# Loading the first tokens of a fused SSM and FFN kernel in two column groups, and turning them in smaller pieces

## The chip, the cores and the metric

The kernel runs on one core of one Trainium2 chip. The metric is the device time of one execution in microseconds (us), taken over several runs. All times "from the start" below are microseconds after the beginning of the span of one profiled execution. Every kernel told of here gave a correct result.

## The reference

`x` has 2048 tokens of 640 features, in bf16. A gate mixes a diagonal state-space model with a feed-forward network:

```python
g = sigmoid((x * gate_w).sum(-1, keepdims=True))
a = A_ref(x, ...)      # SSM with 640 complex states: h[t] = Lam_bar*h[t-1] + B_bar x[t];  y = 2 Re(C h) + D x
h = gelu(x @ w1 + b1)  # w1: 640 x 1728
b = h @ w2 + b2        # w2: 1728 x 640
out = g * a + (1 - g) * b
```

## The kernel before

The tokens are worked off in four chunks of 512. A chunk is four tiles of 128 tokens (`a` = 0 to 3), and the 640 features are five blocks of 128 (`kd` = 0 to 4). The first matrix product of the FFN needs x with features on the partitions. For chunks 1 to 3 a DMA transposes x. For chunk 0 TensorE itself "turns" it: each 128x128 block is multiplied by an identity matrix into a `bank` (a tile in PSUM, the memory that matmuls write to), and VectorE (DVE) or ScalarE (ACT) copies it to `xT[0]`. In this document x0, x1, x2, x3 are the four tiles of chunk 0. `w1a`, `w1b` and `w1c` are the first 768, the next and the last columns of w1. The matmuls on w1a are the work of the first 12 us. They are cut into strips so that they can begin when only some tiles and some feature blocks are there.

The start of the kernel (cuts are marked, the comments are mine):

```python
    load_xn(0, 0, 1)                 # x0, all 640 features, SyncE's queue
    load_w1a(nc.scalar, 0)           # ScalarE's queue
    load_xn(0, 1, 2)                 # x1
    load_w1a(nc.scalar, 2)
    ...                              # two parameter rows on ScalarE's queue
    load_xn(0, 2, 3)
    load_xn(0, 3, 4)
    rows(nc.sync, prmA[2 * KS:3 * KS, :], A_Lambda_re)
    for kd in (1, 4, 3):
        load_w1a(nc.sync, kd)
    ...
    pA = bank()
    for n in (512, 512, 512, 512, 512, 512, 128, 128):      # warm-up matmuls on constants
        nc.tensor.matmul(pA[:, 0:n], lhsT=ones(P), rhs=ones(n), start=True, stop=True)
    ...
    tA, tB = bank(), bank()
    turn(tA, 0, 0, 0)                        # turn(bank, column, tile a, block kd)
    turned(nc.vector, tA, 0, 0, 0, 1)        # copy blocks 0..1 of tile 0 to xT[0]
    for i in range(2):
        turn(tB, i * P, 0, 1 + i)
    turned(nc.vector, tB, 0, 0, 1, 3)
    for i in range(2):
        turn(pA, i * P, 0, 3 + i)
    turned(nc.scalar, pA, 0, 0, 3, 5)
    ...
    strip(0, 0, P, True)                     # six matmuls: block 0, tile 0
    turn_all(1)                              # five turns of tile 1, three copies
    strip(2, 0, P, False)
    strip(0, P, HT, True)
    strip(2, P, HT, False, 0, 3)
    turn_all(2)
    ...
```

A simple model of the clock of each engine (`Clock.pe = 4.2`, the moment at which TensorE's work begins) decides in which order DVE's work is issued later on.

## Time and profile before

| | before |
|---|---|
| median of 3 runs | 215.99 us (215.8 to 216.4) |
| span of the profiled execution | 214.2 us |
| TensorE busy | 98% of the span |
| first turn / first w1a matmul / first w1b matmul | 3.60 / 4.22 / 12.82 us |
| DVE's sine tables ready | 25.7 us |

From the page of the kernel before, the length of the span, the busy time of each engine, and the chain of work that ended last by engine:

```profile
span 214.2 us, 3547 instructions
...
PE 210.0 (98%) x1385; PEld 116.4 (54%) x1385; DVE 188.4 (88%) x385; ACT 103.3 (48%) x185; POOL 1.1 (0%) x12
...
PE 96%; DMA 2%; SPq 0%; ACT 0%; DVE 0%; issue 0%
```

TensorE (PE) bounds the kernel. There is almost nothing to win but the holes at the start. These are in the timeline of PE for the first 13 us; the columns are start, length, engine, line, operation, tiles, shapes, count, and in brackets the idle time before and what ended it:

```profile
0.77 2.93 PE L220 MATMUL bank<-const-bfloat16-1.0 128*128 128x512 bf16 x8 [0.77 <-PEq L716]
3.60 0.46 PE L223 MATMUL bank<-ident,xn 128*128 128x128 bf16 x5
4.22 0.49 PE L258 MATMUL bank<-xT,w1a 128*128 128x128 bf16 x6 [0.16 <-DVE xT L230]
4.96 0.45 PE L223 MATMUL bank<-ident,xn 128*128 128x128 bf16 x5 [0.24 <-DMA xn<-in_A_x_dram]
5.25 1.09 PE L258 MATMUL bank<-xT,w1a 128*128 128x128 bf16 x15
...
7.09 0.17 PE L361 MATMUL bank<-ident,prmA 128*128 128x15 bf16 x1 [0.30 <-ACT xT L232]
...
12.82 0.38 PE L258 MATMUL bank<-xT,w1b 128*128 128x512 bf16 x1
```

Read it so: the warm-up matmuls hold PE to about 3.6 us. Then x0 is turned, and PE waits three times, for DVE's copy, for the DMA of x1, and for ScalarE's copy. After that the brackets show no further wait.

The bracket understates a stop, because a matmul is recorded as longer than the distance to the next start. In a full stream a 128-column matmul starts 55 to 56 ns after the one before it and a 512-column one 216 ns after. I therefore call "stop" the distance between two starts less that figure.

DVE's trigonometric work begins with this operation (timeline of DVE, the same columns):

```profile
8.29 0.82 DVE L370 TENSOR_TENSOR gel<-tf,thp_c 128x640 f32<-128x640 f32 x1
```

It is DVE's first operation on 640 columns; the change halves it.

### The profile page before, as it was taken

How to read it: one execution, taken by the hardware profiler on the slowest of the kernel's cores; microseconds unless marked ns; L12 is line 12 of the kernel's file. 1: busy time of each engine (PE TensorE's matmuls, PEld its weight loads, DVE VectorE, ACT ScalarE, POOL GpSimd, SP SyncE). 2: the span in 40 equal slices, each digit the busy share in tenths (PEclk: the TensorE clock that was granted, in tenths of full speed). 3: DMA queues.
4: the chain of work that ended last, by engine and by line, in shares of the span. 5: the costliest groups of instructions: out<-in, count | busy, mean ns of one | idle time of the engine just before them, and what ended most of it. 6: DMA issues, size and time to landing. Idle time of an engine off the chain costs nothing.

```text
span 214.2 us, 3547 instructions
## 1 busy us (share of the span) xinstructions
PE 210.0 (98%) x1385; PEld 116.4 (54%) x1385; DVE 188.4 (88%) x385; ACT 103.3 (48%) x185; POOL 1.1 (0%) x12
## 2 busy tenths in 40 slices
PE   7999999999999999999999999999999999999994
PEld 3745444454454644775445577444455567664773
DVE  2899999999998999998999999899999999973153
ACT  3599956675867697203573210456682422304200
POOL 1000000000000000000000000000000000000000
PEclk9999999999999999999999999999999999999999
DMA  6899999995000000061000006100000000100011
GB/s 200 238 189 182 187 250 314 257 212 136 3 0 0 3 0 2 12 186 62 0 0 3 0 0 185 63 0 0 2 3 14 0 3 31 61 34 0 0 66 61
DMA packets 31059, 15.84 MB, mean 74 GB/s; under 512 B 22978, under 2 KB 31042, under 8 KB 31042
## 3 DMA queue, kind: packets, MB, share of 16 engines
q1 hardware_dynamic: 30590, 15.18, 29.1%
q10 hardware_dynamic: 452, 0.43, 0.6%
q8 instruction: 11, 0.18, 0.3%
q14 instruction: 6, 0.05, 0.1%
HBM read 7.48 MB, written 2.62 MB: 47 GB/s over the span
## 4 chain that ended last, share of the span: by engine, by line
PE 96%; DMA 2%; SPq 0%; ACT 0%; DVE 0%; issue 0%
PE bank L598 27%; PE bank L258 26%; PE bank L657 20%; PE bank L540 20%; DMA xn<-in_A_x_dram 2%; PE bank L614 1%; PE bank L284 1%; PE bank L223 0%; SPq L122 0%; ACT xT L232 0%; DVE ot L662 0%; PE bank L361 0%; PE bank L274 0%; PE bank L390 0%
## 5 line engine op out<-in xcount | busy, mean ns | idle before, releaser
L598 PE MATMUL bank<-w_sb,gel 128*128 128x512 bf16 (+1 forms) x416 | 57.9, 299 | 0.0
L598 PEld LDWEIGHTS <-gel 128*128 128x128 bf16 x416 | 32.3, 98 | 25.5
L543 ACT ACTIVATE bu<-bank 128x512 bf16<-128x512 f32 x40 | 23.6, 608 | 37.3 <-PE bank L540 36.7
L263 ACT ACTIVATE gel<-bank,colB 128x512 bf16<-128x512 f32 x52 | 33.9, 696 | 11.7 <-PE bank L258 11.4
L657 PEld LDWEIGHTS <-hs 128*128 128x128 bf16 x330 | 31.6, 98 | 11.5
L494 DVE TENSOR_TENSOR_SCAN g<-r_c,carry,v 128x512 bf16<-128x512 f32 x30 | 37.3, 1271 | 0.0
L606 ACT ACTIVATE gb<-bank,gcol 128x512 f32<-128x512 f32 (+1 forms) x32 | 15.1, 527 | 33.5 <-PE bank L614 17.3
L258 PE MATMUL bank<-xT,w1a 128*128 128x512 bf16 (+1 forms) x156 | 27.6, 329 | 0.2 <-DVE xT L230 0.2
L657 PE MATMUL bank<-CT_im,hs 128*128 128x320 bf16 (+2 forms) x165 | 27.1, 295 | 0.0
L657 PE MATMUL bank<-CT_re,hs 128*128 128x320 bf16 (+2 forms) x165 | 27.1, 295 | 0.0
L662 DVE SCALAR_TENSOR_TENSOR ot<-bank,gcol,gb 128x320 bf16<-128x320 f32 (+2 forms) x33 | 17.6, 535 | 10.8 <-PE bank L657 10.0
L540 PE MATMUL bank<-xT,BT_re 128*128 128x512 bf16 x100 | 24.8, 379 | 0.0
L540 PE MATMUL bank<-xT,BT_im 128*128 128x512 bf16 x100 | 24.8, 379 | 0.0
L258 PEld LDWEIGHTS <-w1a 128*128 128x128 bf16 x156 | 13.4, 97 | 13.0 <-issue 0.7
L573 DVE TENSOR_TENSOR bank<-xn,Dbc 128x320 f32<-128x320 bf16 (+2 forms) x33 | 14.6, 483 | 3.9 <-ACT gb L606 3.8
L258 PE MATMUL bank<-xT,w1b 128*128 128x512 bf16 x80 | 17.9, 379 | 0.0
L540 PEld LDWEIGHTS <-BT_im 128*128 128x128 bf16 x100 | 9.8, 98 | 11.8
L475 DVE TENSOR_TENSOR v<-wa,wb 128x512 bf16<-128x512 bf16 x40 | 15.2, 421 | 0.6
L540 PEld LDWEIGHTS <-BT_re 128*128 128x128 bf16 x100 | 9.7, 98 | 11.0
L587 ACT ACTIVATE bank<-b2bc 128x512 f32<-128x512 bf16 (+1 forms) x24 | 11.7, 529 | 7.3 <-DVE ot L662 7.3
L475 DVE TENSOR_TENSOR wa<-TCOS,g 128x1024 bf16<-128x1024 bf16 x20 | 13.7, 686 | 0.1
L258 PE MATMUL bank<-xT,w1c 128*128 128x512 bf16 x60 | 13.7, 379 | 0.0
(101 smaller groups left out, 164.2 us busy)
## 6 DMA issues: line engine op xcount, KB each, us to landing
out_dram<-ot SPq DMA_DIRECT2D x15, 160.0 KB, 1.8
w_sb<-in_B_w_dram SPq DMA_DIRECT2D x1, 2080.0 KB
xn<-in_A_x_dram SPq DMA_DIRECT2D x2, 640.0 KB
xn<-in_A_x_dram SPq DMA_DIRECT2D x4, 160.0 KB, 3.7
w1b<-in_B_w_dram SPq DMA_DIRECT2D x5, 128.0 KB, 3.1
xn<-in_A_x_dram SPq DMA_DIRECT2D x2, 320.0 KB, 3.7
w1a<-in_B_w_dram SPq DMA_DIRECT2D x3, 192.0 KB, 3.0
w1c<-in_B_w_dram SPq DMA_DIRECT2D x5, 112.0 KB, 3.5
```

The lines of the kernel that those rows point to most:

```text
L258: nc.tensor.matmul(p[:, t0:t1], lhsT=w, rhs=xT[c][:, kd, t0:t1], start=(kd == 0) if first is None else first, stop=(kd == last), skip_grou ...
L263: nc.scalar.activation(out=gel[c][:, kf, :], in_=p[:, :], func=ACT.Gelu_apprx_tanh, bias=b1_c[:, kf:kf + 1])
L475: nc.vector.tensor_tensor(out=o, in0=a, in1=b, op=op)
L494: nc.vector.tensor_tensor_scan(s["g"][:, ri, :], r_c[:, ks:ks + 1].to_broadcast([P, CH]), s["v"][:, ri, :], init, ALU.mult, ALU.add)
L540: nc.tensor.matmul(p[:], lhsT=BT[ks >= KSA][:, kd, (ks % KSA if ks < KSA else ks - KSA) * P:][:, 0:P], rhs=xT[c][:, kd, :], start=(kd == 0 ...
L543: nc.scalar.activation(out=bu[:, ri, :], in_=p[:], func=ACT.Identity)
L573: dve_now(ck.pe, 0.45, lambda: nc.vector.tensor_tensor(out=p[:, 0:d1 - d0], in0=xn[c][:, a, d0:d1], in1=Dbc[:, d0:d1], op=ALU.mult))
L587: nc.scalar.activation(out=v, in_=src, func=ACT.Identity)
L598: nc.tensor.matmul(p[:, col:col + d1 - d0], lhsT=gel[c][:, kf, a * P:(a + 1) * P], rhs=w2_sb[:, kf, d0:d1], start=False, stop=False, skip_ ...
L606: nc.scalar.activation(out=gbs[ti][:, d0:d1], in_=p[:, col:col + d1 - d0], func=ACT.Identity, scale=gcol[:, 1, ti:ti + 1])
L657: nc.tensor.matmul(p[:, 0:d1 - d0], lhsT=hs[c][:, j, lo:lo + P], rhs=CT[:, j % KS, d0:d1], start=False, stop=(j == 2 * KS - 1), skip_group ...
L662: nc.vector.scalar_tensor_tensor(out=ot[:, d0:d1], in0=p[:, 0:d1 - d0], scalar=gcol[:, 0, ti:ti + 1], in1=gbs[ti][:, d0:d1], op0=ALU.mult, ...
```

## The change

The intent is to feed PE sooner. Of each tile, features 0 to 255 come first (64 KB instead of 160 KB), then the other 384 features of two tiles at a time. More of the copies out of PSUM go to ScalarE. The parameter rows leave ScalarE's queue. Sines are computed for 64 positions instead of 128, with one more doubling by the addition theorem. Chunk 3's x also comes in one DMA instead of two (not shown). The core of the diff, with cuts:

```diff
-    load_xn(0, 0, 1)
+    load_x0(nc.sync, 0, 1, 0, KA * P)            # KA = 2: features 0..255 of tile 0
     load_w1a(nc.scalar, 0)
-    load_xn(0, 1, 2)
-    load_w1a(nc.scalar, 2)
+    load_x0(nc.sync, 1, 2, 0, KA * P)
+    load_w1a(nc.scalar, 1)
+    load_x0(nc.sync, 2, 3, 0, KA * P)
+    load_x0(nc.scalar, 0, H, KA * P, D)          # features 256..639 of tiles 0 and 1
+    load_x0(nc.sync, 3, 4, 0, KA * P)
+    load_w1a(nc.sync, 2)
 ...                                              # three parameter rows now on SyncE's queue
+    load_x0(nc.sync, H, TPC, KA * P, D)
+    nc.sync.dma_start(out=w1a34[:], ...)         # w1a 3 and 4 in one DMA
 ...
-    HC = CH // 4
+    HC = CH // 8
 ...
-        pe = 4.2
+        pe = 3.4
 ...
+    def turn_first(a, other):
+        t = bank()
+        turn(t, 0, a, 0)
+        turned(nc.vector, t, 0, a, 0, 1)
+        turn(other, a * P, a, 1)
+        turned(nc.scalar, other, a * P, a, 1, 2)
+
+    turn_first(0, pA)
+    turn_first(1, bank())
 ...
+    part(0, 0)                                   # part(kd, a): six matmuls of block kd, tile a
+    part(0, 1)
+    turn_first(2, pA)
+    part(1, 0)
+    turn_first(3, pA)
+    part(1, 1)
+    part(0, 2)
+    turn_rest(0, ((KA, KD, bank(), nc.scalar),))
+    part(1, 2)
 ...
+    part(0, 3)
+    turn_rest(1, ((KA, KD, bank(), nc.vector),))
+    part(1, 3)
+    turn_rest(2, ((KA, KD, pA, nc.scalar),))
+    part(2, 0)
 ...
+    turn_rest(3, ((KA, KA + 1, bank(), nc.vector), (KA + 1, KD, pA, nc.scalar)))
 ...
+    part(2, 1)
+    part(2, 2)
+    part(2, 3)
 ...
-    double(HC, 3)
+    double(HC, 4)
+    double(2 * HC, 3)
```

More of the change, by code (lines that the diff above doesn't have):

```diff
@@ L83 @@
     xT = [const.tile([P, KD, CH], BF16, name=f"xT{c}") for c in range(NCH)]
-    w1a = [const.tile([P, cut1], BF16, name=f"w1a_{kd}") for kd in range(KD)]
+    w1a = [const.tile([P, cut1], BF16, name=f"w1a_{kd}") for kd in range(3)]
+    w1a34 = const.tile([P, 2, cut1], BF16, name="w1a34")
+    w1a += [w1a34[:, j, :] for j in range(2)]
     w1b = [const.tile([P, cut2 - cut1], BF16, name=f"w1b_{kd}") for kd in range(KD)]
@@ L128, in rows, with load_x0 @@
         queue.dma_start(out=dst, in_=v.rearrange("(j p) -> j p", p=P))
-    load_xn(0, 0, 1)
-    load_w1a(nc.scalar, 0)
-    load_xn(0, 1, 2)
-    load_w1a(nc.scalar, 2)
+    KA = 2
+    xn[0] = xnp.tile([P, TPC, D], BF16, name="xn")
+    def load_x0(queue, a0, a1, d0, d1):
+        queue.dma_start(out=xn[0][:, a0:a1, d0:d1], in_=x2d[a0 * P:a1 * P, d0:d1].rearrange("(a p) d -> p a d", p=P))
+    load_x0(nc.sync, 0, 1, 0, KA * P)
+    load_w1a(nc.scalar, 0)
+    load_x0(nc.sync, 1, 2, 0, KA * P)
[4 more added lines that the diff above has]
+    load_w1a(nc.sync, 2)
     nc.vector.memset(prmA[:], 0.0)
     nc.vector.memset(prmB[:], 0.0)
-    rows(nc.scalar, prmA[0:KS, :], A_log_dt)
-    rows(nc.scalar, prmA[KS:2 * KS, :], A_Lambda_im)
     warm = const.tile([P, 1], F32, name="warm")
     nc.scalar.activation(out=warm[:], in_=nc.const_aps.tensor(1.0, [P, 1], BF16), func=ACT.Exp)
-    load_xn(0, 2, 3)
-    load_xn(0, 3, 4)
+    rows(nc.sync, prmA[0:KS, :], A_log_dt)
+    rows(nc.sync, prmA[KS:2 * KS, :], A_Lambda_im)
     rows(nc.sync, prmA[2 * KS:3 * KS, :], A_Lambda_re)
-    for kd in (1, 4, 3):
-        load_w1a(nc.sync, kd)
+    load_x0(nc.sync, H, TPC, KA * P, D)
+    nc.sync.dma_start(out=w1a34[:], in_=B_w1[3 * P:KD * P, 0:cut1].rearrange("(k p) f -> p k f", p=P))
     rows(nc.sync, prmB[KS:NB, :], B_b1[0:(KF - 1) * P])
@@ L155 @@
     nc.gpsimd.memset(b1x[:, F_LAST:F_LAST + 1], 0.0)
-    NQ = 4
+    NQ = 5
     spans = const.tile([P, NQ], F32, name="spans")
-    for i, m in enumerate((1.0, float(CH), float(CH // 2), float(CH // 4))):
+    for i, m in enumerate((1.0, float(CH), float(CH // 2), float(CH // 4), float(CH // 8))):
         nc.gpsimd.memset(spans[:, i:i + 1], m)
@@ L232, in turned @@
             nc.scalar.activation(out=dst, in_=src, func=ACT.Identity)
-    tA, tB = bank(), bank()
-    turn(tA, 0, 0, 0)
-    turned(nc.vector, tA, 0, 0, 0, 1)
-    for i in range(2):
-        turn(tB, i * P, 0, 1 + i)
-    turned(nc.vector, tB, 0, 0, 1, 3)
-    for i in range(2):
-        turn(pA, i * P, 0, 3 + i)
-    turned(nc.scalar, pA, 0, 0, 3, 5)
+    def turn_first(a, other):
[6 more added lines that the diff above has]
+    turn_first(1, bank())
     def col(name, dtype=F32, n=KS):
@@ L318, in strip, with turn_rest @@
             ff1_mm(banks[kf], 0, kf, kd, t0, t1, first, 3)
-    def turn_all(a, last=False):
-        tB = bank()
-        for i in range(3):
-            turn(tB, i * P, a, i)
-        turned(nc.vector, tB, 0, a, 0, 1)
-        turned(nc.scalar if last else nc.vector, tB, P, a, 1, 3)
-        for i in range(2):
-            turn(pA, i * P, a, 3 + i)
-        if not last:
-            turned(nc.scalar, pA, 0, a, 3, 5)
+    def turn_rest(a, parts):
+        for k0, k1, t, engine in parts:
+            for k in range(k0, k1):
+                turn(t, (k - k0) * P, a, k)
+            turned(engine, t, 0, a, k0, k1)
     HB = CH // 2
@@ L352, in over, with part @@
         return c.rearrange("p (k o) -> p k o", o=1).to_broadcast([P, KS, n])
-    strip(0, 0, P, True)
-    turn_all(1)
-    strip(2, 0, P, False)
-    strip(0, P, HT, True)
-    strip(2, P, HT, False, 0, 3)
-    turn_all(2)
-    strip(2, P, HT, False, 3, FA)
-    nc.tensor.matmul(pA[:, HT:HT + 3 * KS], lhsT=prmA[:], rhs=ident[:, 0:3 * KS], start=True, stop=True, skip_group_check=True)
-    nc.vector.tensor_copy(out=colA[:], in_=pA[:, HT:HT + 3 * KS])
+    def part(kd, a):
+        strip(kd, a * P, (a + 1) * P, kd == 0)
+    part(0, 0)
[7 more added lines that the diff above has]
+    part(1, 2)
+    nc.tensor.matmul(pA[:, 0:3 * KS], lhsT=prmA[:], rhs=ident[:, 0:3 * KS], start=True, stop=True, skip_group_check=True)
+    nc.vector.tensor_copy(out=colA[:], in_=pA[:, 0:3 * KS])
     nc.scalar.activation(out=dt16[:], in_=ldt_c, func=ACT.Exp)
     nc.vector.tensor_scalar(out=limp[:], in0=lim_c, scalar1=INV_2PI, scalar2=None, op0=ALU.mult)
-    strip(0, HT, HT + P, True)
-    turn_all(3, True)
+    part(0, 3)
[3 more added lines that the diff above has]
+    part(2, 0)
     nc.vector.tensor_tensor(out=dtl[:], in0=dt16[:], in1=lre_c, op=ALU.mult)
     nc.vector.tensor_tensor(out=thp_c[:], in0=dt16[:], in1=limp[:], op=ALU.mult)
+    turn_rest(3, ((KA, KA + 1, bank(), nc.vector), (KA + 1, KD, pA, nc.scalar)))
     nc.scalar.activation(out=r_c[:], in_=dtl[:], func=ACT.Exp)
     nc.vector.tensor_tensor(out=u, in0=tf[:].rearrange("p (o i) -> p o i", o=1).to_broadcast([P, KS, HC]), in1=over(thp_c[:], HC), op=ALU.mult)
-    turned(nc.vector, pA, 0, 3, 3, 5)
     nc.vector.tensor_copy(out=kk[:], in_=u)
     nc.vector.tensor_tensor(out=red, in0=u, in1=kk[:], op=ALU.subtract)
-    strip(2, HT, HT + P, False)
-    strip(0, HT + P, CH, True)
-    strip(2, HT + P, CH, False)
-    strip(1, 0, CH, False)
+    part(2, 1)
+    part(2, 2)
+    part(2, 3)
     nc.scalar.activation(out=FS[:, :, 0:HC], in_=red, func=ACT.Sin, scale=TWO_PI_M)
@@ L690 @@
     fin_a(1)
-    load_xn(3, 0, H)
-    load_xn(3, H, TPC)
+    load_xn(3)
     ssm(3)
```

## The prediction

> **What bounds the kernel now.** TensorE. The page shows PE busy 98% of 214.2 us; the chain that ended last is 96% PE, unbroken from about 7.1 us. Only the start has holes: in the timeline of PE, warm-up matmuls run to about 3.6 us, the first real ones (five turns of tile 0) start at 3.60 when its 160 KB have landed, the first w1a matmul at 4.22, and until 7.1 us PE waits 0.16 (turn copy), 0.24 (second tile's DMA) and 0.30 us (ScalarE copy), about 0.8 us in all. The first w1b matmul starts at 12.82. The change touches the first 13 us: it can win about 1 us.
>
> **What it does, costed.**
> - *First loads.* Tile 0 is 64 KB instead of 160. In the packet records its packets (55 ns each) took from 1.77 to 3.02 us, alternating with w1a's 65 ns packets; landing was 0.5 us later.[...] So smaller x packets (estimate 25 ns) help less than their bytes say: estimate x0 landed at 3.0, x1 at 3.7 (was 4.95). But warm-ups hold PE to about 3.5, and the first w1a matmul stands behind both tiles' turns: 3.8 to 4.0 instead of 4.22.
> - *PE work.* 24 matmuls of 128 columns replace 6 of 512: 24 x 0.06 - 6 x 0.216 = +0.15 us.
> - *Turn buffers.* Most turns share one spare bank and pA, and wait for the copies out of them: gaps of 0.1 us at the third and fourth tiles, about 0.3 us at the last turns (a 384-column copy, 0.5 us, behind only 7 matmuls).
> - *Rows on SyncE, paired w1a.* Their issues wait on earlier landings, but all land before PE needs them.
>
> Sum: first w1b matmul at 12.2 to 12.4: 0.4 to 0.6 us won.
>
> **DVE.** Four ops of 640 columns halve; six of 320 are added.[...] The tables, done at 25.6, will be done 1.5 to 2 us later, though the sines end earlier. DVE has no gap from 15 to 63 us, then gaps of 0.96 (fold), 0.44 and 0.88 us (waits for PE at 92 and 98). These and a changed order of DVE work (the schedule model starts PE 0.8 us earlier) should absorb the lateness before it reaches PE; seeds of the second output stage (1.8 us ahead at 121) are nearest.
>
> **Predicted time.** 215.4 us (215.99 before), 8 in 10 between 214.8 and 216.1. Faster by over 2%: 0.01; within: 0.98; slower: 0.01.
>
> **What will show it.** Timeline of PE: first turn at 3.4 to 3.6, first w1a matmul 3.8 to 4.0, first w1b matmul 12.2 to 12.4, turns waiting for copies about 0.4 us. DVE's tables end at 27 to 27.6. Thereafter every PE piece of the chain of waits keeps its length, shifted alike; PE busy stays near 210.
>
> **What would make it wrong.** The second tile lands before 3.4 us (up to 0.9 won); the spare bank stalls PE more, or ScalarE's turns and table load delay a copy (all lost); DVE's lateness reaches a seed or hs before an output stage (PE gaps at 86 to 98 or 121 to 126 us, up to 1 us slower).

The estimate of 25 ns for a row of 512 B lies on the line through the measured 55 ns for 1280 B and 65 ns for 1536 B. On DVE the terms came to about 1.2 us saved and 2.7 us added; "1.5 to 2 us later" is what is left of them. By the traces a two-tensor fp32 operation takes 0.82 us on 640 columns (before) and 0.48 to 0.49 us on 320 (after), the cast among the four 0.48 and 0.33 us, which makes 1.2 us saved and 2.9 us added. That issues on SyncE's queue wait on earlier landings is in the trace of before: 1.2 us for a w1a block and 0.4 us for an x tile.

## The result

| | before | after |
|---|---|---|
| median of the 4 runs of the same rounds | 215.93 us (215.8 to 216.4) | 216.28 us (215.97 to 216.5) |
| ratio after / before, 95% interval | | 1.0011 (0.9992 to 1.0031) |
| span of the profiled execution | 214.2 us | 214.4 us |
| first turn / first w1a / first w1b | 3.60 / 4.22 / 12.82 us | 3.50 / 4.25 / 13.06 us |
| first w1b matmul to the end of the span | 201.4 us | 201.4 us |
| DVE's tables ready | 25.7 us | 28.5 us |

A ratio here is the mean time of one kernel's fast runs over the mean of the other's fast runs of the same rounds, so it is not quite the ratio of the medians. The change did nothing that can be told from zero; I had expected 215.4. All outputs are right. The page of the kernel after:

```profile
span 214.4 us, 3572 instructions
...
PE 209.4 (98%) x1384; PEld 117.9 (55%) x1403; DVE 189.4 (88%) x389; ACT 103.6 (48%) x188; POOL 1.0 (0%) x13
...
PE 96%; DMA 1%; issue 1%; ACT 0%; SPq 0%; DVE 0%
```

The timeline of PE of the kernel after:

```profile
0.77 2.93 PE L230 MATMUL bank<-const-bfloat16-1.0 128*128 128x512 bf16 x8 [0.77 <-PEq L728]
3.50 0.96 PE L233 MATMUL bank<-ident,xn 128*128 128x128 bf16 x4
4.25 1.49 PE L268 MATMUL bank<-xT,w1a 128*128 128x128 bf16 x12
5.53 0.40 PE L233 MATMUL bank<-ident,xn 128*128 128x128 bf16 x2
...
9.33 0.27 PE L233 MATMUL bank<-ident,xn 128*128 128x128 bf16 x2 [0.19 <-ACT xT L242]
...
13.06 1.24 PE L268 MATMUL bank<-xT,w1b 128*128 128x512 bf16 x5
```

Two things differ from the prediction. The first w1a matmul is at 4.25, not at 3.8 to 4.0, since the second pair of turns (in the group of four at 3.50) starts only at 4.06, when x1 has landed (its DMA has signalled that it is complete). And twelve w1a matmuls take 1.49 us here, while fifteen of them took 1.09 us before. The starts in that group are 107 ns apart. That is half rate, and it lasts to 5.77 us; in the trace of before full rate began at 3.65 us. The column of the granted clock on the page doesn't show this; it reads 9 from the first slice on. The spacing of the matmuls does.

The stop at 9.33 is foreseen (0.3 us) and about right: the distance between the starts is 407 ns, a stop of 0.35. It waits for this copy by ScalarE (timeline of ACT):

```profile
8.79 0.49 ACT L242 ACTIVATE xT<-bank 128x384 bf16<-128x384 f32 x1 [0.62 <-PE bank L233]
```

On DVE, the first of the halved operations starts later than before, since it stands in DVE's order behind the copy of the last but two of the turns (timeline of DVE):

```profile
9.18 0.29 DVE L240 CAST xT<-bank 128x128 bf16<-128x128 f32 x1 [0.19 <-PE bank L233]
9.39 0.48 DVE L384 TENSOR_TENSOR gel<-tf,thp_c 128x320 f32<-128x320 f32 x1
```

From the first w1b matmul to the end of the span both kernels take 201.4 us (214.225 - 12.820 and 214.447 - 13.057). So the tables that DVE finishes 2.8 us later cost nothing, and whatever happened, happened in the first 13 us.

### The profile page after: what moved, and what is told of

Read it like the earlier page. It is cut to its first block, busy times and chain, and to the rows that moved or that the text cites. A ratio compares the mean times of both kernels' runs of the same rounds, so it can differ in the third digit from the quotient of the medians.

```text
span 214.4 us, 3572 instructions
## 1 busy us (share of the span) xinstructions
PE 209.4 (98%) x1384; PEld 117.9 (55%) x1403; DVE 189.4 (88%) x389; ACT 103.6 (48%) x188; POOL 1.0 (0%) x13
## 4 chain that ended last, share of the span: by engine, by line
PE 96%; DMA 1%; issue 1%; ACT 0%; SPq 0%; DVE 0%
PE bank L611 26%; PE bank L268 26%; PE bank L670 20%; PE bank L553 20%; DMA xn<-in_A_x_dram 1%; PE bank L627 1%; PE bank L294 1%; PE bank L233 1%; ACT xT L242 0%; SPq L136 0%; DVE ot L675 0%; PE bank L284 0%; PE bank L402 0%; PE bank L371 0%
## 5 line engine op out<-in xcount | busy, mean ns | idle before, releaser
L611 PE MATMUL bank<-w_sb,gel 128*128 128x128 bf16 (+1 forms) x408 | 57.1, 297 | 0.6 <-issue 0.3
L268 PE MATMUL bank<-xT,w1a 128*128 128x512 bf16 (+1 forms) x170 | 28.2, 318 | 0.2
L268 PEld LDWEIGHTS <-w1a 128*128 128x128 bf16 x174 | 14.8, 102 | 11.4
```

Of the source, the lines that this page charges most:

```text
L268: nc.tensor.matmul(p[:, t0:t1], lhsT=w, rhs=xT[c][:, kd, t0:t1], start=(kd == 0) if first is None else first, stop=(kd == last), skip_grou ...
L611: nc.tensor.matmul(p[:, col:col + d1 - d0], lhsT=gel[c][:, kf, a * P:(a + 1) * P], rhs=w2_sb[:, kf, d0:d1], start=False, stop=False, skip_ ...
```

## The experiments

My first theory was: *the early stage is now cut by waits for copies, and these can be undone (late turn, sines)*. The rivals: *half rate at the start costs the changed kernel more than the kernel before, since it begins real work sooner*; and *the loads do not come sooner, so no order of turns helps*.

### The two kernels again

The same two files, unchanged, on other chips. `after_again` and `before_again`:

> The changed kernel once more, unaltered. Clock theory: the moment when TensorE goes from half to full rate falls at a different place in each execution (5.77 us in the trace on record of after, 3.65 in that of before), and the changed kernel pays about half of every microsecond of delay between 4.1 and 6 us. So if this trace goes to full rate near 3.7 us, its first w1b matmul starts at 12.2 to 12.4 us and the time is about 215.5; at 5.8 us, 13.0 to 13.1 and about 216.3; at 6.8 us, about 13.5 and 216.7. Rival (the new order of loads is slower whatever the clock): first w1b matmul at 13.0 to 13.1 wherever the clock changes.

> The kernel before once more. Clock theory: at 3.7 us its first w1b matmul starts at 12.8 as on record; at 5.8 us at about 13.2, at 6.8 us at about 13.6: it also loses, but less per microsecond, because it waits more for data in that time. Rival: 12.8 wherever the clock changes.

Measured: after 216.15 us (215.56 to 216.65), 0.9992 of before (0.9972 to 1.0012); before against itself 216.33 us, 1.000 (0.998 to 1.002). The spread of one kernel, 1.1 us, is larger than all I look for. In this trace of the changed kernel full rate begins at 3.42 us, and the timeline of PE shows the start without the half rate:

```profile
4.21 0.29 PE L233 MATMUL bank<-ident,xn 128*128 128x128 bf16 x2 [0.46 <-DMA xn<-in_A_x_dram]
4.33 1.08 PE L268 MATMUL bank<-xT,w1a 128*128 128x128 bf16 x12
...
12.67 4.48 PE L268 MATMUL bank<-xT,w1b 128*128 128x512 bf16 x20
```

The same twelve matmuls take 1.08 us instead of 1.49, stop included, and w1b begins 0.39 us sooner than in the trace on record, although w1a began 0.08 later. (The expectation's "half of every microsecond" was an estimate; the trace on record had 1.67 us more of half rate after 4.1 us, and lost 0.39.) So the trace on record was an unlucky one. But x1 is still not there before 4.2 us.

The second trace of *before* is as telling. From its timeline of PE:

```profile
4.28 0.80 PE L258 MATMUL bank<-xT,w1a 128*128 128x128 bf16 x6
4.87 0.58 PE L223 MATMUL bank<-ident,xn 128*128 128x128 bf16 x5
...
12.86 0.38 PE L258 MATMUL bank<-xT,w1b 128*128 128x512 bf16 x1
```

Here half rate lasts to about 5.1 us (by the spacing), the six w1a matmuls take 0.80 us instead of 0.49, and the turns of x1 follow without any wait. x1 landed at 4.43 us here and at 4.91 in the trace on record, though its last row came at 3.98 and 4.03. So the wait of 0.40 us for x1, which the change was to remove, was largely a late landing in the one trace that I had. And w1b begins only 0.04 us later than there, because the slow matmuls fill time that was lost anyway.

A third look at the changed kernel, on yet another chip:

> The changed kernel a third time, so that the next three have it beside them on the same chip. Pooled over the chips so far it is within 0.2 us of the kernel before; I expect that again, with first w1a matmul at 4.2 to 4.35 us.

Measured: 216.10 us (215.97 to 216.20), ratio 1.0005 (0.999 to 1.002). Together the three sets of the changed kernel (15 runs) have a mean of 216.16 us, and the runs of before of the same rounds (26) one of 216.15 us. The difference is 0.0 us; by the spread of the runs it is known to about 0.2 us either way.

This third trace is at full rate from 3.60 us on. PE waits in it for x1 (a stop of 0.38 us) and once more for x2, 0.40 us. From its timeline of PE:

```profile
5.48 0.28 PE L233 MATMUL bank<-ident,xn 128*128 128x128 bf16 x2 [0.24 <-DMA xn<-in_A_x_dram]
```

### The last turns later

```diff
-    turn_rest(3, ((KA, KA + 1, bank(), nc.vector), (KA + 1, KD, pA, nc.scalar)))
+    turn_rest(3, ((KA, KA + 1, bank(), nc.vector),))
 ...
     part(2, 1)
+    turn_rest(3, ((KA + 1, KD, pA, nc.scalar),))
     part(2, 2)
```

> The changed kernel with the last two turns of tile 3 behind six more matmuls of w1a's third part. The trace of after shows PE stopped for 0.35 us there (9.0 to 9.33 us), waiting for ScalarE's copy of 384 columns out of the same bank. If that stop is on the critical path, 0.3 to 0.35 us less than the changed kernel at the same moment of the clock (about 215.9 against 216.27), first w1b matmul 12.7 at 5.8 us. Rival: something later (sines, colB) holds the w1b start, no gain.

Measured: 215.95 us (215.59 to 216.14), ratio 0.9985 (0.9967 to 1.0003). The stop of 0.35 us before the last turns is gone from the timeline of PE, where they now stand at 9.03, and w1b begins at 12.42 us although half rate lasted to 4.86:

```profile
9.03 0.27 PE L233 MATMUL bank<-ident,xn 128*128 128x128 bf16 x2
```

The stop is real and can be avoided by order alone. The median is 0.20 us under `after_again` on the same chip, where I had expected 0.3 to 0.35, and the interval still reaches to 1.

### Sines for 128 positions in the new order

```diff
-    HC = CH // 8
+    HC = CH // 4
 ...
-    double(HC, 4)
-    double(2 * HC, 3)
+    double(HC, 3)
```

> The changed kernel with sines for 128 positions again (one doubling fewer, as before). My theory says that VectorE's work is not on the critical path: the same time as the changed kernel within 0.1 us at the same moment of the clock, though VectorE's tables end about 1.5 us earlier. Rival (VectorE's lateness reaches TensorE somewhere): 0.3 us or more faster.

Measured: 216.38 us (216.19 to 216.56), ratio 1.0002 (0.9985 to 1.0018). I expected no effect on PE, and that was wrong. The timeline of PE:

```profile
12.77 0.38 PE L268 MATMUL bank<-xT,w1b 128*128 128x512 bf16 x1
13.37 4.34 PE L268 MATMUL bank<-xT,w1b 128*128 128x512 bf16 x19 [0.22 <-DVE w1c L405]
```

The second w1b matmul starts 0.60 us after the first instead of 0.22: it needs a bank that DVE has still to empty, and DVE's small copies stand behind the sine work. In all, first w1b to the end of the span took 201.84 us here and 201.4 or 201.5 in every other trace. By this one trace, halving the sines is worth about 0.45 us *in the new order*; the medians on the same chip differ by 0.23. It pays for a delay that the new order itself gives DVE. In the old order 640 columns fitted without a stop.

### Everything on hand before PE begins (a failed design)

I wanted to see the order of PE's work alone. Before the first load I put long memsets on DVE, and gave PE 28 warm-up matmuls of which the second part reads ones from a tile. By mistake I took a tile that a late DMA fills.

```diff
+    wones = Dbc[:, 0:P]
+    nc.vector.memset(w2_sb[:], 0.0)
 ...
+    for n in (512,) * 12:
+        nc.tensor.matmul(pA[:, 0:n], lhsT=wones, rhs=ones(n), start=True, stop=True)
```

> The kernel before with every load held back by about 7 us (by fills on VectorE ahead of them) and the warm-up matmuls made long enough that TensorE is at full rate before the first turn in every execution. About 223 us. If the moment of the clock and nothing else spreads the times of one kernel (215.6 to 216.9 so far), these stay within about 0.3 us of each other; if other things spread them, over 1 us as before. First w1b matmul 12.1 us after the first load's issue (12.82 - 0.73 on record).

> The changed kernel held back in the same way: the comparison of the two without the clock. After_again, at full rate from 3.42 us, started w1b at 12.67 us against 12.82, so I expect first w1b 11.9 to 12.0 us after the first load's issue and 0.1 to 0.2 us less than the held-back kernel before. If the slow clock had taken the whole of my predicted gain, it would be 0.5 to 0.6 us less; if the change is worth nothing, the same.

Measured: 265.27 us (before's order) and 265.36 us (after's). PE stood still until 48.6 and 48.0 us, lost full rate and regained it only at 51.3 and 52.4. The totals answer nothing that was asked. The pair still shows one thing: all loads were long there when PE went on, and from the first turn to the first w1b matmul the old order took 8.78 us and the new one 8.69. With no load to wait for, the two orders differ by 0.1 us in this pair of traces.

### The clock taken out

The same design mended: warm-ups that last until the loads arrive, with ones from a tile that only DVE writes. PE is at full rate from the first turn on: five turns take 0.45 us for before (0.71 in `before_again`, at half rate), and twelve w1a matmuls 1.08 us for after (1.49 in the trace on record).

```diff
+    wones = gelN[0][:, 0, :]
 ...
+    for n in (512,) * 20:
         nc.tensor.matmul(pA[:, 0:n], lhsT=ones(P), rhs=ones(n), start=True, stop=True)
+    for n in (512,) * 12:
+        nc.tensor.matmul(pA[:, 0:n], lhsT=wones, rhs=ones(n), start=True, stop=True)
```

> The held-back kernel before again, with its mistake mended (in the first try the second half of the warm-up read a tile that a late load fills, and TensorE stood still for 40 us). About 223 us. All warm-ups end before the first tile lands and TensorE is at full rate at the first turn. First w1b matmul 12.1 us after the first load's issue. If the moment of the clock is what spreads the times, they now stay within 0.4 us of each other.

> The changed kernel held back in the same way, with the same mending. Clock theory with late x1: w1b 11.9 to 12.0 us after the first load's issue, 0.1 to 0.2 us less than held_before, clear of noise if the spread shrinks. If nothing but the clock took my predicted gain: 0.5 to 0.6 us less. If the loads give nothing: equal.

Measured: 222.94 us (222.72 to 223.40) for before and 223.09 us (223.06 to 223.17) for after, four runs each; ratios 1.0326 and 1.0331. The issue of the first load came at 7.84 us in the one and at 8.02 in the other (the second memset is 592 columns wide in one and 640 in the other), so the 0.15 us between the totals say nothing. Timelines of PE, first of before, then of after:

```profile
10.65 0.45 PE L235 MATMUL bank<-ident,xn 128*128 128x128 bf16 x5
11.27 0.49 PE L270 MATMUL bank<-xT,w1a 128*128 128x128 bf16 x6 [0.16 <-DVE xT L242]
...
19.55 0.81 PE L270 MATMUL bank<-xT,w1b 128*128 128x512 bf16 x3
```

```profile
10.82 0.27 PE L244 MATMUL bank<-ident,xn 128*128 128x128 bf16 x2
11.33 0.29 PE L244 MATMUL bank<-ident,xn 128*128 128x128 bf16 x2 [0.24 <-DMA xn<-in_A_x_dram]
11.45 1.08 PE L279 MATMUL bank<-xT,w1a 128*128 128x128 bf16 x12
...
16.17 0.27 PE L244 MATMUL bank<-ident,xn 128*128 128x128 bf16 x2 [0.19 <-ACT xT L253]
...
19.89 0.38 PE L279 MATMUL bank<-xT,w1b 128*128 128x512 bf16 x1
```

From the issue of the first load, the first w1b matmul comes after 11.71 us in the one and 11.88 in the other. I had expected 0.1 to 0.2 us less for the change, and 0.5 to 0.6 if only the clock had taken its gain. So without the clock the change gains nothing either: the loss of the gain is not the clock's. The stops of these two traces, and of two others that ran at full rate from the first turns on, can be added up, in us:

| stop (distance between starts less the normal one) | before | before, clock held | after again | after, clock held |
|---|---|---|---|---|
| first w1a waits for DVE's copy | 0.32 | 0.32 | 0 | 0 |
| turns of x1 wait for its DMA | 0.40 | 0.09 | 0.62 | 0.40 |
| parameter matmul waits for ScalarE's copy | 0.47 | 0.47 | 0 | 0 |
| sixth w1a matmul waits for ScalarE's copy | 0 | 0 | 0.25 | 0.25 |
| turns of x3 wait for the bank | 0 | 0 | 0.16 | 0 |
| turns of x2 and x3 wait for their DMAs | 0 | 0 | 0 | 0.23 |
| last turns wait for ScalarE's copy | 0 | 0 | 0.35 | 0.35 |
| others | 0.28 | 0.28 | 0.05 | 0.05 |
| sum | 1.47 | 1.16 | 1.43 | 1.28 |

The waits moved, and their sum stayed. In the third trace of the changed kernel it is 1.59, of which 0.79 is for the DMAs of x1 and x2.

### No warm-up matmuls

```diff
-    for n in (512, 512, 512, 512, 512, 512, 128, 128):
-        nc.tensor.matmul(pA[:, 0:n], lhsT=ones(P), rhs=ones(n), start=True, stop=True)
```

> The kernel before without its eight warm-up matmuls. TensorE first works at 3.6 us[...]. I expect about 1 us more than the kernel before (about 217), w1b at about 13.8.

> The changed kernel without warm-up matmuls. Clock theory (the changed kernel gives TensorE dense work from 4.1 us on, and so pays more per microsecond at half rate): 1.2 to 1.4 us more than the changed kernel (about 217.4), 0.2 to 0.4 more than nowarm_before. Rival (both pay alike): the same difference as with warm-ups, 0 to 0.2 us less than nowarm_before.

Measured: before without warm-up 217.47 us (217.29 to 217.78), ratio 1.0071; after without it 217.30 us (216.55 to 217.91), ratio 1.0064. Full rate began at 9.2 and 8.2 us (3.65 and 5.77 in the traces on record). Timeline of PE of the two, first before:

```profile
14.42 0.81 PE L256 MATMUL bank<-xT,w1b 128*128 128x512 bf16 x3
```

```profile
4.35 1.44 PE L266 MATMUL bank<-xT,w1a 128*128 128x128 bf16 x12
...
14.09 4.48 PE L266 MATMUL bank<-xT,w1b 128*128 128x512 bf16 x20
```

Both kernels pay for a late full rate, 1.5 us against before on the same chip and 1.2 us against the changed kernel on other chips. I had expected the changed kernel to come out 0.2 to 0.4 us above the other here, and it came out 0.2 below: my theory that it pays more falls. The clock moved the times of both kernels here; it didn't favour one of them.

### x1 on the other queue

The packet records show why x1 was late. Each tile comes as 128 rows, eight for each of the core's 16 DMA engines if they are spread evenly. The records don't name the tile or the engine of a row; I tell the tiles apart by order.

| | rows of x | time of a row | first to last row of x1 | of w1a's first block |
|---|---|---|---|---|
| before | 1280 B | 55 ns | 2.98 to 4.03 us | 1.93 to 3.34 us |
| after | 512 B | 27 ns | 2.77 to 3.56 us | 1.86 to 3.11 us |
| x1 on the other queue | 512 B | 27 ns | 1.85 to 2.59 us | 2.24 to 3.51 us |

Eight rows of 27 ns are 0.22 us of work, but x1 took 0.79 us. If it shares each engine with w1a on the other queue, whose rows of 1536 B take 65 ns, the sum is 8 x (27 + 65) = 0.74 us. For before, 8 x (55 + 65) = 0.96 us, and it took 1.05. This fits engines that take turns between the two queues. (Whether they do so after each row or after several, the sums don't tell. At the very start it fits less: beside x0 on the other queue x1 took 0.74 us, where 8 x (27 + 27) = 0.43.) So the load of x1 had fewer bytes by 60% but took only 25% less time. And it stood behind x0 on its queue, whose rows beside w1a's took 1.04 us. I moved x1 to 3 to ScalarE's queue, beside x0, and w1a behind x0:

```diff
     load_x0(nc.sync, 0, 1, 0, KA * P)
-    load_w1a(nc.scalar, 0)
-    load_x0(nc.sync, 1, 2, 0, KA * P)
-    load_w1a(nc.scalar, 1)
-    load_x0(nc.sync, 2, 3, 0, KA * P)
-    load_x0(nc.scalar, 0, H, KA * P, D)
-    load_x0(nc.sync, 3, 4, 0, KA * P)
+    load_x0(nc.scalar, 1, 2, 0, KA * P)
+    load_w1a(nc.sync, 0)
+    load_x0(nc.scalar, 2, 3, 0, KA * P)
+    load_w1a(nc.sync, 1)
+    load_x0(nc.scalar, 3, 4, 0, KA * P)
+    load_x0(nc.sync, 0, H, KA * P, D)
```

> The changed kernel with tiles 0 and 1 on two queues at once, ahead of every w1a load (tiles 1 to 3 on ScalarE's queue, w1a on SyncE's). My theory: x1 was late (4.0 to 4.2 us instead of my 3.7) because its packets take turns with w1a's longer ones. Then x1 lands at about 3.1 us, the second tile's turns follow the first's at 3.7 us without a wait, first w1a matmul at 4.1 instead of 4.25 to 4.33, w1b 0.2 us earlier at the same moment of the clock. Rival[...]: x1 still lands at 3.7 us or later.

Measured: 216.08 us (215.53 to 216.42), ratio 1.0001 (0.9984 to 1.0018). x1 was turned without a wait, at 3.71 us, right behind x0 at half rate. The timeline of PE:

```profile
3.50 0.63 PE L233 MATMUL bank<-ident,xn 128*128 128x128 bf16 x4
```

The first w1a matmul started at 4.19, 0.06 us sooner than in the trace on record; half rate lasted to 6.0 here, and w1b began at 12.97. This move changes two things at once: x1 stands first on its queue, and it stands beside x0 instead of w1a. Its rows still took 0.74 us (0.79 before the move); they began at 1.85 us instead of 2.77.

The same loads with the last turns later and a shorter warm-up, `best`:

```diff
-    for n in (512, 512, 512, 512, 512, 512, 128, 128):
+    for n in (512, 512, 512, 512, 512, 128):
```

> Tiles first, the late last turns, and 1 us less of warm-up (five of 512 columns and one of 128, ending near 3.0 us). First turn at about 3.1, first w1a matmul at 3.75, w1b at 11.8 us if TensorE is at full rate by 3.7 us and 12.2 to 12.3 if at 5.8 us; 215.2 us median, 0.8 to 1 us under the kernel before. If the clock takes most of it, 215.7.

Measured: 215.66 us (215.19 to 217.23), ratio 0.999 (0.9964 to 1.0017). The timeline of PE:

```profile
2.96 0.63 PE L233 MATMUL bank<-ident,xn 128*128 128x128 bf16 x4
4.43 0.84 PE L268 MATMUL bank<-xT,w1a 128*128 128x128 bf16 x12 [0.84 <-DMA w1a<-in_B_w_dram]
```

Now the turns are done by 3.6 us, and PE waits 0.84 us for w1a. The wait has moved from x1 to w1a.

### w1a's first block over both queues

So I halved the first block of w1a and gave each queue one half, behind x0 and x1. `loads_only` is this with the order of the changed kernel and the shorter warm-up:

```diff
     load_x0(nc.sync, 0, 1, 0, KA * P)
-    load_w1a(nc.scalar, 0)
-    load_x0(nc.sync, 1, 2, 0, KA * P)
-    load_w1a(nc.scalar, 1)
+    load_x0(nc.scalar, 1, 2, 0, KA * P)
+    half_w1a0(nc.sync, 0, cut1 // 2)
+    half_w1a0(nc.scalar, cut1 // 2, cut1)
     load_x0(nc.sync, 2, 3, 0, KA * P)
-    load_x0(nc.scalar, 0, H, KA * P, D)
-    load_x0(nc.sync, 3, 4, 0, KA * P)
+    load_x0(nc.scalar, 3, 4, 0, KA * P)
+    load_w1a(nc.sync, 1)
+    load_x0(nc.sync, 0, H, KA * P, D)
 ...                                              # and the shorter warm-up
```

> The changed kernel with its order on TensorE untouched but other loads: tiles 0 and 1 on two queues first, then w1a's first part split over both queues, and 1 us less warm-up. Theory: first w1a matmul at 3.6 to 3.8 us instead of 4.25 to 4.33, which my prediction had at 3.8 to 4.0; 0.3 to 0.5 us less than after_third, less where the clock is late. Rival: w1a lands no earlier than 4.2 us because the bytes ahead of it are the same, and nothing is gained.

Measured: 216.65 us (216.46 to 216.80), ratio 1.003 (1.0016 to 1.0044); slower than the changed kernel on the same chip by 0.55. The timeline of PE:

```profile
3.86 1.38 PE L272 MATMUL bank<-xT,w1a 128*128 128x128 bf16 x12 [0.27 <-DVE xT L244]
...
5.95 0.51 PE L272 MATMUL bank<-xT,w1a 128*128 128x128 bf16 x6 [0.59 <-DMA w1a<-in_B_w_dram]
...
13.33 4.48 PE L272 MATMUL bank<-xT,w1b 128*128 128x512 bf16 x20
```

This time the first w1a matmul does start at 3.86, as I had predicted for the change. But the second block of w1a now lands at 5.90 us, and what was won at 3.86 is lost there, and more. Half rate lasted to 5.03 here; that is not what cost the time, since PE stood waiting for the block after it.

`no_stalls` has the loads of the changed kernel and takes two stops out of PE's order: the last turns are later, and both turns of x1 go to one bank before either is copied. `best2` is this order with the loads and the short warm-up of `loads_only`.

```diff
-    def turn_first(a, other):
+    def turn_first(a, other=None):
         t = bank()
+        other = other or t
         turn(t, 0, a, 0)
-        turned(nc.vector, t, 0, a, 0, 1)
         turn(other, a * P, a, 1)
+        turned(nc.vector, t, 0, a, 0, 1)
         turned(nc.scalar, other, a * P, a, 1, 2)
 ...
-    turn_first(1, bank())
+    turn_first(1)
 ...                                              # and the last turns later, as above
```

> The changed kernel with its loads untouched, without the two stops for bank copies: the late last turns, and both turns of tile 1 in one bank, so that the sixth w1a matmul waits for no ScalarE copy. At full rate the traces show these stops as 0.35 and 0.25 us. Theory: they are on the critical path and took back what the order saved; first w1a matmul unchanged (4.2 to 4.35), from it to the first w1b 7.8 us instead of 8.34 to 8.44, and 0.3 to 0.5 us less than after_third. Rival (the late first matmul alone is to blame, the stops only fill time in which data are missing): 0 to 0.1 us.

> Both together. If the two losses are separate and each as large as the traces say: first w1b at 11.5 to 11.7 us at full rate, 12.0 to 12.2 with a late clock; median 215.2, 0.7 to 0.9 us less than after_third and than the kernel before. If they hide behind each other: about 215.6.

Measured: `no_stalls` 215.57 us (215.11 to 216.15), ratio 0.9984 (0.9968 to 1.0001), 0.53 us under the changed kernel on the same chip. `best2` 216.25 us (216.05 to 217.78), ratio 1.0025 (1.0001 to 1.0049): 0.68 slower with these loads and the shorter warm-up than without, the second block of w1a again late (0.92 us of idle time before 5.86). From the timelines of PE, first of `no_stalls`, then of `best2`:

```profile
4.19 0.92 PE L269 MATMUL bank<-xT,w1a 128*128 128x128 bf16 x12
...
9.04 0.27 PE L233 MATMUL bank<-ident,xn 128*128 128x128 bf16 x2
...
12.43 4.48 PE L269 MATMUL bank<-xT,w1b 128*128 128x512 bf16 x20
```

```profile
5.86 0.51 PE L273 MATMUL bank<-xT,w1a 128*128 128x128 bf16 x6 [0.92 <-DMA w1a<-in_B_w_dram]
```

The two stops are gone in `no_stalls`: the twelve matmuls take 0.92 us instead of 1.08, and the turns at 9.04 stand behind nothing. It is not free of stops: at 5.79 PE waits 0.40 us for x2. w1b begins 0.24 us sooner than in the best trace of the changed kernel.

### The best order, once more and with x1 on the other queue

`no_stalls_again` is unchanged; `tiles_first` is the same order and the full warm-up with the loads of `x_first`.

> The changed kernel without the stops for bank copies, a second time. If the 0.53 us under the changed kernel and 0.41 us under the kernel before are the stops' worth and not the chip's luck: again 0.3 to 0.5 us under the kernel before (215.5 where that is 215.95).

> The same, with tiles 1 to 3 on ScalarE's queue and w1a on SyncE's, as in x_first, and the full warm-up. Its second tile waits for nothing; w1a's first part lands at 3.8 to 4.4 us, the second at about 5. If data decide what is left: within 0.15 us of no_stalls_again either way, with the wait moved from x tiles to w1a. If the second tile is what holds the start: 0.2 us or more faster.

Measured: `no_stalls_again` 215.88 us (215.63 to 216.13), ratio 0.9994 (0.9979 to 1.0008); `tiles_first` 215.65 us (215.15 to 215.71), ratio 0.998 (0.9965 to 0.9995). The second set of `no_stalls` is 0.1 us under before, not the 0.3 to 0.5 I had expected; its trace was at half rate to 6.28 us. Both sets together (12 runs) have a mean of 215.77 us, and before on this chip one of 216.05 (12 runs). `tiles_first` is the only version whose interval lies wholly under 1, but 11 of the 12 runs of before in it are from the earlier call. Timeline of PE:

```profile
4.41 1.11 PE L269 MATMUL bank<-xT,w1a 128*128 128x128 bf16 x12 [0.28 <-DMA w1a<-in_B_w_dram]
...
12.45 4.48 PE L269 MATMUL bank<-xT,w1b 128*128 128x512 bf16 x20
```

Its median is 0.34 us under that of these 12 runs. It has not been timed beside the changed kernel itself. Even here PE waits for w1a at the start.

## Why the prediction was right or wrong

**Right: what bounds the kernel, and where the change can act.** From the first w1b matmul to the end every trace of the changed order took 201.4 or 201.5 us, but for the one with the long sines (201.84). The size class (within 2%) follows from that.

**Right: DVE's lateness is harmless.** The tables ended at 28.5 us, 1 us later than I said, since the first halved operation stood behind one more copy (9.39 instead of 8.29 us). That none of it reached PE is shown by the 201.4 us; which gap of DVE absorbed it I did not look up. The fp32 multiplications of two tensors took 0.82 us on 640 columns and 0.48 on 320, so half the columns took 59% of the time. What I did not see is that with long sines the new order would have cost 0.45 us.

**Right: the last turns' stop,** 0.3 us predicted and 0.35 measured. **Too large, but small: PE's added work.** I put 0.15 us for it. At the measured spacing it is 24 x 0.056 - 6 x 0.216 = 0.05.

**Wrong, the main step: "x1 at 3.7 (was 4.95)", and from it "the first w1a matmul ... 3.8 to 4.0 instead of 4.22".** x1 was turned at 4.06 in the trace on record and at 4.21 and 4.04 in the others of the same kernel, and the first w1a matmul started at 4.25, 4.33 and 4.16. That is no gain, where I had put 0.2 to 0.4 us. I had read the alternation of the two queues in the trace, and relied on it. The traces fit such turn-taking (0.74 us summed and 0.79 measured for x1, 0.96 and 1.05 for that of before), but don't show how many rows make a turn. I did reckon with it: 8 x (25 + 65) ns are 0.72 us a tile, which from a first row at 1.77 us, and with 0.5 us of landing, gives the 3.0 and 3.7 that I wrote. The term that failed is the time of the rows. In the trace on record x0's took 1.04 us instead of 0.72, and x1's 0.79; so x1's last row came at 3.56 us instead of 3.21 (3.49 and 3.41 in the other traces), and landing took 0.45 us more (0.67 and 0.58). Why x0's rows take longer than their sum at the very start, no run here shows. Where x1 was first on the other queue it was turned at 3.17 to 3.71 us, without a wait. This shows that its place, behind x0 on a queue beside the one with w1a, made it late; it doesn't separate the two.

Also the other side of the comparison was off. "Was 4.95" came from one trace, where x1 landed 0.88 us after its last row. In the second trace of before it landed 0.45 us after it, and the turns of x1 did not wait at all; with the clock held they waited 0.09 us. Of the holes of 0.8 us that I listed, the "0.24 us (second tile's DMA)" was mostly not there to be won.

And the repair shows the deeper fault, in the path: I took x1 as the thing to wait for. The first w1a matmul needs w1a as well. With x1 early, w1a's first block landed at 3.8 to 4.4 us (`x_first`, `best`, `tiles_first`), and in the two later cases PE waited for it; with both early, its second block landed at 5.81 and 5.90 (`best2`, `loads_only`). In `after_third`, `no_stalls` and the changed kernel with the clock held, PE waited for x2 or x3 as well. PE waits for whichever of these loads comes last, and each move put another one last.

**Wrong in size: "gaps of 0.1 us at the third and fourth tiles, about 0.3 us at the last turns".** The stops for banks and copies came to 0.81 and 0.65 us in the two traces of the table, not 0.4 to 0.5. The one that I had missed is the sixth w1a matmul, which waits 0.25 us for ScalarE's copy of x1's second part. Together with the wait for x1, the changed kernel stops as long as the kernel before (the table of stops: 1.43 and 1.28 against 1.47 and 1.16). Taking the two avoidable stops out lowered the mean to 0.28 us under before over both calls, and to 0.44 us (the median to 0.53) under the changed kernel in the one call that had both.

**Not foreseen: the clock at the start.** I assumed full rate from the first turn. The traces show 107 and 56 ns between 128-column matmuls at half and full rate, and in the clock records one stretch of full rate, of 211.626 us from 3.65 us on in the trace of before and of 208.213 us from 5.77 us on in that of after. What sets the exact moment, no run here shows; without warm-up matmuls it came later, at 9.2 and 8.2 us. In the traces with the full or the shortened warm-up and the normal start, full rate began anywhere from 3.4 to 6.3 us. In the trace on record half rate lasted to 5.77 us and made the stage from w1a to w1b 8.81 us long, where the second trace has 8.34. This is why 13.06 stood there instead of 12.67. But it can hit both kernels, though in the second trace of before it cost only 0.04; and the pair with the clock held shows the same missing gain. It explains why two traces of one kernel differ, not why the change gained nothing.

**What stays open.** The time from the last row of a load to its landing varied from 0.2 to 0.9 us between loads and traces, and with it the wait for x1 (0 to 0.40 us with the loads of before, 0.17 to 0.62 with those of after, over all traces). No run here tells what sets it. The pair with the clock held spread unequally, 0.68 us for before and 0.11 for after, without a cause that I can show. And whether `no_stalls` is worth 0.1 or 0.5 us is within the noise of these runs.

## What to carry to other kernels

Here the first matmuls needed several loads, and cutting one of them smaller or moving it forward moved the wait to the next (with x1 early, PE waited 0.84 us for w1a in `best`). In such a case ask for each load when its last row can come, given what stands on the other queue, and follow it through to the last operand. Before counting a removed wait as won, see in a second trace whether it is there each time, and list the new ones: what stands behind each copy out of PSUM, and which two turns share a bank. And where the gain sought is under 0.5% (the 1.1 us by which the runs of one kernel spread here), find the moment of full clock in each trace from the spacing of the matmuls, and pool runs from several chips before believing a difference.

## Other figures of these traces

- From the last row of a load to its landing it took 0.2 us (first block of w1a, before and after) to 0.9 us (x1 of before), and for the same load of the same kernel 0.45 us in one trace and 0.88 in another. About 1 us lay between the start of the issue and the first row (0.73 to 1.77 us for x0 in the trace of before).
- A single row took 27, 36, 55 and 65 ns for 512, 768, 1280 and 1536 B (medians of the traces of before and after).
- The ACT_TABLE_LOADs took 1.28 us. In the trace of after the next activation followed at once, and so did the load itself after the activation before it (an activation to 10.12 us, the load from 10.13 to 11.42, the next activation at 11.43).
